# Gate and value products of three hidden blocks moved between the attention stages of the first half chunk, with fewer identity products

## The chip, the cores and the metric

The kernel runs on one core of one Trainium2 chip. The metric is the device time of one execution in microseconds (us); the median of three runs of the kernel before is 1180.62. The engines are named PE (TensorE, the matrix products), DVE (VectorE), ACT (ScalarE), POOL (GpSimd) and SP (SyncE, which issues the DMAs here). Each works through its own queue in order.

## What is computed

Eight sequences of 512 local and 32 global tokens, eight heads of 64. A local token attends to the local tokens within 32 places and to the global tokens; a global token attends to all. The output of attention, 4608 tokens of 512 numbers, goes through a gated feed-forward layer with 1536 hidden numbers:

```python
s_ll = np.where(mask, s_ll, -1000000000.0)
s_l = np.concatenate([s_lg, s_ll], axis=-1)
out_l = np.matmul(sm(s_l), np.concatenate([v_g, v_l], axis=2))
out_g = np.matmul(sm(s_g), v_all)
...
gate = 1.0 / (1.0 + np.exp(-(x @ w_gate)))
val = x @ w_val
return (gate * val @ w_out).astype(np.float32)
```

The three weights are given as 64-bit floats.

## The kernel before

The tokens are worked in chunks: the first sequence in two half chunks of 256 tokens (chunk 0 and chunk 1), the other sequences as chunks of 512, the global tokens as a last one. For each chunk attention makes x, and `ffn_stream` then runs over items (chunk, f), where f is one of 12 blocks of 128 hidden numbers. An item takes 12 gate products and 12 value products (hi times hi, lo times hi, hi times lo, each over four tiles kt of the 512 inputs, since numbers are split in a high and a low part), then tanh, minimum, exponential and merging on ACT and DVE, which give hh; then the output products with wo into the PSUM banks bank_o. The order of items begins with blocks 0 to 7 of chunk 0, then blocks 0 to 7 of chunk 1, then both by turns.

The order of everything is written by hand as a table of events with due times. `ffn_stream` yields after each step with the step's length in units of four products of 512 columns, and the events whose time has come are written out between. Events with times far below zero come before the first item: the attention of chunk 0 runs from -1000 on, four units for each head. A scheduler then moves instructions a little by its own estimate, within the dependences.

Attention of one head in chunk 0 (`local_unit`) has four stages: the scores on PE (L234) with the mask and minimum on DVE (L248) and the exponential on ACT (L251); the normalization on DVE (L218); the transposes on PE (L270), with a copy on ACT (L278); the products with v on PE (L293, L294), with a copy to x on ACT (L297). After every second head `x_split` (L372, L373) makes the high and low part of one kt tile of x. In chunk 0 `fill` adds products of the identity matrix with itself (L110) after the scores, after the transposes and after the products with v; nobody reads them.

The weights are converted on the chip. `stage` loads 512 KB of 64-bit words into one of three buffers; `convert` makes 32-bit floats of them (ACT L137, DVE L139 and L140), casts them to the high part (ACT L141) and subtracts for the low part (POOL L142), then stages the third load after it. Gate and value weights stay in SBUF; those for the output go to DRAM (L153, L154) and come back as wo for each item (L428). Their high and low parts share two buffers (tag kl). `CONVERT_EARLY` sets the times of block 0's three conversions, `CONVERT` the first time and the step of the others.

## Time and profile before

| | us |
|---|---|
| median of 3 runs | 1180.62 |
| lowest and highest | 1178.43, 1186.85 |
| the profiled execution | 1179.81 |
| its span, from the first to the last instruction | 1177.9 |

The profile is of one execution. A row of its timeline has the start and the length in us, engine, line, operation, what is written from what, the shapes and the count, and in brackets the idle time of the engine before it with what ended that. A product of 32-bit floats that are not split stands as two records. A row on DMAs has the count, the size of each and the median time from issue to landing. PE counts as busy while a product is on its way, so a busy PE isn't PE at its peak. The granted clock of PE is 1.00 throughout.

### The profile page before, as it was taken

The numbers are of one execution on the slowest core, as the hardware profiler recorded it, in microseconds if no ns is written. First come the engines' busy times: TensorE is split into PE (matmuls) and PEld (weight loads), VectorE is DVE, ScalarE is ACT, GpSimd is POOL, SyncE is SP. The second block draws the span as 40 slices with busy tenths as digits, with TensorE's granted clock in tenths as the row PEclk, the third lists the DMA queues.
The fourth block names the chain that finished last, engine by engine and source line by source line (L and its number), as shares of the span: only waits on it lengthen the run. The fifth ranks groups of instructions, "written<-read, shape, count | busy, mean of one in ns | idle before, by whom it ended". The sixth has DMA issues, their size and how long they took to land.

```text
span 1177.9 us, 19115 instructions
## 1 busy us (share of the span) xinstructions
PE 1146.4 (97%) x6596; PEld 962.3 (82%) x6596; DVE 773.7 (66%) x2132; ACT 753.2 (64%) x1737; POOL 413.3 (35%) x408
## 2 busy tenths in 40 slices
PE   8999999999999999999999999999999999999998
PEld 7777788888888888888888888888888888888897
DVE  5677657577676677667676677667676677533343
ACT  5898877566675676666675676666675675532343
POOL 2444435334353444334352444334452443100000
PEclk9999999999999999999999999999999999999999
DMA  8888844333443343343343343343344342122143
GB/s 295 283 288 279 259 134 128 95 116 94 115 116 113 106 115 98 106 140 90 113 115 114 105 116 98 107 149 91 103 116 122 99 118 81 44 100 72 54 151 118
DMA packets 59489, 151.81 MB, mean 129 GB/s; under 512 B 6144, under 2 KB 19456, under 8 KB 59392
## 3 DMA queue, kind: packets, MB, share of 16 engines
q1 hardware_dynamic: 59392, 150.59, 42.2%
q8 instruction: 52, 0.85, 0.3%
q14 instruction: 45, 0.37, 0.1%
HBM read 135.36 MB, written 15.20 MB: 128 GB/s over the span
## 4 chain that ended last, share of the span: by engine, by line
PE 75%; DVE 11%; ACT 8%; issue 3%; DMA 2%; POOL 1%; SPq 0%; ACTq 0%; DVEq 0%; POOLq 0%
PE bank_v L400 20%; PE bank_g L400 19%; PE bank_o L437 19%; PE bank_x L234 4%; DVE p_buf L218 4%; PE bank_y L270 4%; ACT s_sb L251 3%; PE bank_x L301 2%; PE bank_x L302 2%; PE bank_x L318 2%; PE bank_x L361 1%; DVE bank_v L420 1%; DVE bank_v L421 1%; PE bank_o L110 1%; ACT hh L423 1%
## 5 line engine op out<-in xcount | busy, mean ns | idle before, releaser
L400 PE MATMUL bank_v<-xt,wv 128*128 128x512 f32 (+1 forms) x1440 | 328.3, 364 | 14.1 <-DVE pt L282 14.1
L400 PE MATMUL bank_g<-xt,wg 128*128 128x512 f32 (+1 forms) x1440 | 330.4, 364 | 0.1
L437 PE MATMUL bank_o<-wo,hh 128*128 128x512 f32 x1224 | 329.2, 400 | 1.2 <-ACT hh L423 1.2
L400 PEld LDWEIGHTS bank_v<-xt,wv 128*128 128x128 f32 x1440 | 237.1, 189 | 51.0 <-issue 16.0
L400 PEld LDWEIGHTS bank_g<-xt,wg 128*128 128x128 f32 x1440 | 236.8, 189 | 37.4 <-issue 2.5
L437 PEld LDWEIGHTS bank_o<-wo,hh 128*128 128x128 f32 x1224 | 217.2, 189 | 41.8 <-ACT hh L423 3.0
L251 ACT ACTIVATE s_sb<-s_sb,nm 128x192 f32<-128x192 f32 (+1 forms) x240 | 110.4, 462 | 98.2 <-DVE nm L248 97.3
L218 DVE TENSOR_SCALAR p_buf<-s_sb,r 128x128 f32<-128x128 f32 (+2 forms) x443 | 153.5, 383 | 6.6 <-PE bank_y L270 1.7
L306 POOL TENSOR_TENSOR x<-t 64x256 f32<-64x256 f32 x104 | 76.4, 735 | 172.1 <-DVE t L305 146.1
L211 POOL TENSOR_TENSOR vhl<-v_raw,vhl 128x512 fp32r<-128x512 f32 x52 | 67.2, 1293 | 187.4 <-ACT vhl L210 104.1
L198 POOL TENSOR_TENSOR kl<-qk_raw,qk_hi 128x704 fp32r<-128x704 f32 x52 | 88.6, 1703 | 108.3 <-ACT qk_hi L197 107.8
L423 ACT CAST hh<-bank_v 128x512 fp32r<-128x512 f32 (+1 forms) x120 | 62.7, 522 | 96.1 <-DVE bank_v L421 95.2
L408 ACT ACTIVATE th<-bank_g 128x512 f32<-128x512 f32 (+1 forms) x120 | 63.7, 531 | 87.0 <-PE bank_g L400 86.6
L413 DVE TENSOR_SCALAR mn<-bank_g 128x512 f32<-128x512 f32 (+1 forms) x108 | 67.4, 624 | 71.8 <-ACT th L408 71.8
L305 DVE TENSOR_TENSOR t<-bank_x,t 64x512 f32<-64x512 f32 x104 | 70.7, 680 | 62.0 <-ACT t L304 61.1
L420 DVE TENSOR_TENSOR bank_v<-bank_v,mn 128x512 f32<-128x512 f32 (+1 forms) x120 | 73.6, 614 | 53.5 <-PE bank_v L400 48.4
L248 DVE CUSTOM_DVE_ANT_0 s_sb<-bank_x,masks 128x192 f32<-128x192 f32 (+1 forms) x240 | 79.9, 370 | 38.5 <-PE bank_x L234 35.6
L424 DVE TENSOR_TENSOR hh<-bank_v,hh 128x512 fp32r<-128x512 f32 (+1 forms) x120 | 73.0, 608 | 35.1 <-ACT hh L423 33.2
L200 POOL TENSOR_TENSOR qk_hi<-qk_raw,qk_hi 64x256 fp32r<-64x256 f32 x104 | 80.3, 792 | 4.1
L421 DVE SCALAR_TENSOR_TENSOR bank_v<-th,bank_v 128x512 f32<-128x512 f32 (+1 forms) x120 | 73.2, 610 | 1.8
L414 ACT ACTIVATE mn<-mn 128x512 f32<-128x512 f32 (+1 forms) x108 | 62.9, 583 | 12.9 <-DVE mn L413 8.2
L270 PE MATMUL bank_y<-ident,p_buf 128*128 128x128 f32 x440 | 69.7, 274 | 1.3 <-ACT mn L410 0.5
(108 smaller groups left out, 1648.7 us busy)
## 6 DMA issues: line engine op xcount, KB each, us to landing
wo<-wo_dram SPq DMA_DIRECT2D x116, 512.0 KB, 3.4
qk_raw<-in_qk_dram SPq DMA_DIRECT2D x104, 312.0 KB, 4.4
v_raw<-in_v_dram SPq DMA_DIRECT2D x52, 256.0 KB, 2.6
out_dram<-ob SPq DMA_DIRECT2D x34, 256.0 KB, 2.9
xt<-in_w_gate_dram SPq DMA_DIRECT2D x12, 512.0 KB, 5.4
xt<-in_w_val_dram SPq DMA_DIRECT2D x12, 512.0 KB, 5.0
xt<-in_w_out_dram SPq DMA_DIRECT2D x12, 512.0 KB, 5.3
v_nat<-in_v_dram SPq DMA_DIRECT2D x8, 512.0 KB, 7.6
```

What stands on the lines that cost most here:

```text
L198: nc.gpsimd.tensor_tensor(kl, t[:, K0:Q1], hi[:, K0:Q1].bitcast(F32), op=ALU.subtract)
L200: nc.gpsimd.tensor_tensor(hi[64:128, r], t[64:128, r], hi[64:128, r].bitcast(F32), op=ALU.subtract)
L218: nc.vector.tensor_scalar(out, in_, by, None, op0=ALU.mult)
L248: anchor[0] = nc.vector.tensor_tensor_reduce(out=s_sb[:, i, w], in0=s_ps[:, i, w], in1=mid[:, w], scale=-0.125, scalar=3.0e38, op0=ALU.add ...
L251: exp_at[0] = nc.scalar.activation(s_sb[:, i, w], s_sb[:, i, w], AF.Exp, bias=nm[:, i:i + 1], scale=-1.0, accum_out=sm[:, i:i + 1])
L270: nc.tensor.transpose(pt_ps[:, t], flat[:, t * P:(t + 1) * P], ident)
L306: nc.gpsimd.tensor_tensor(dst, t0[:, :, 0], t0[:, :, 1], op=ALU.add)
L400: nc.tensor.matmul(acc, w[a][:, t, fs], xt[:, c, t, x0:x0 + ntok], start=n == 0, stop=n == 11)
L420: nc.vector.tensor_tensor(acc, acc, mn, op=ALU.mult)
L421: nc.vector.scalar_tensor_tensor(acc, th, 1.0, acc, op0=ALU.add, op1=ALU.mult)
L423: nc.scalar.copy(hh[:, 0, 0:ntok], acc)
L437: nc.tensor.matmul(o_ps[t], ph[:, a, t * P:(t + 1) * P], pwo[:, c], start=f2 == 0 and i == 0, stop=f2 == NF - 1 and i == 2)
```

## The change

Line numbers move: L110 becomes L112, L137 L156, L139 and L140 L158 and L159, L141 L160, L142 L161, L153 and L154 L172 and L173, L218 L237, L234 L254, L248 L269, L251 L272, L270 L291, L278 L297, L293 and L294 L312 and L313, L372 L389, L400 L478, L428 L430, L437 L447. The new line L409 is a product of a portion.

- `fill` is called twice only: two products at the start and seven after the scores of head 1, tied behind given instructions. Before, it was eight at the start and one after each of three stages of each head.
- For blocks 0, 1 and 2 of chunk 0 gate and value products are taken out of `ffn_stream`. `pre_products` writes them in portions of six (one kt tile: three gate products, three value products), each tied behind the last attention product written before it. A portion goes into one bank, gate in one half and value in the other: block 0 in bank_o2, block 1 in bank_o3, block 2 in bank_o1. At the start a product with a tile of zeros clears each of them.
- `ffn_stream` begins with the gating of these three blocks (`gate_parts`, `merge`), then item 3; the output products of blocks 0 and 1 come after item 3's gate products, those of block 2 after its value products. Each item from 3 to 20 yields 0.5 more.
- The conversions stand in a new order: gate and value of blocks 0, 1, 2 first (`PRE_AT`), their output weights later (`PRE_OUT`), and from block 3 on by `CONVERT`, which begins one unit earlier at block 3 where it began with block 0. The loads follow that order.

```diff
-FILL = (8, 1)
+FILL = (2, 7)
-CONVERT = (-2, 4, 1, 3)
-CONVERT_EARLY = (-985, -980, -977)
+CONVERT = (-3, 4, 1, 3)
+PRE = 3
+PRE_AT = (-992.9, -991.5, -987.5, -985, -983.2, -979.2)
+PRE_OUT = (-971.5, -967.5, -2)
...
+    zero = spl.tile([P, 512], F32R, name="zero", tag="kl")
+    nc.vector.memset(zero.bitcast(F32), 0.0)
+    pre_banks = []
+    for i in (2, 3, 1)[:PRE]:
+        bank = ps.tile([P, 2, 256], F32, name=f"bank_o{i}")
+        nc.tensor.matmul(bank.rearrange("p a c -> p (a c)"), zero[:, 0:P], zero, start=True, stop=False)
+        pre_banks.append(bank)
+    last_fill = fill(FILL[0])
...
-        if T["first"]:
-            fill(FILL[1])
+        if T["first"] and h == 1:
+            with tc.issue_after(m.ins):
+                fill(FILL[1])
...
+    def pre_products(f, kt):
+        C = chs[0]
+        ntok, x0, xt = C["ntok"], C["x0"], C["xt"]()
+        fs = slice(f * P, (f + 1) * P)
+        bank = pre_banks[f]
+        for i, w in enumerate((wg, wv)):
+            for n, (a, c) in enumerate(((0, 0), (1, 0), (0, 1))):
+                with tc.issue_after(pe_at[0].ins):
+                    nc.tensor.matmul(bank[:, i], w[a][:, kt, fs], xt[:, c, kt, x0:x0 + ntok],
+                                     start=False, stop=kt == KT - 1 and i == 1 and n == 2)
...
+    def load_wo(f):
+        t = ffn.tile([P, 2, DM], F32R, name="wo", bufs=2)
+        nc.sync.dma_start(t.bitcast(F32), wo_dram[f])
+        return t
...
+        wos = {f: load_wo(f) for f in range(2)}
+        for f in range(PRE):
+            half = slice(256 * (f % 2), 256 * (f % 2) + 256)
+            bank = pre_banks[f]
+            hh = hhs[f // 2][:, :, half]
+            gate_parts(bank[:, 0], th[:, half], mn[:, half], f % 2)
+            merge(bank[:, 1], th[:, half], mn[:, half], hh)
+            pend.append((chs[0], f, hh, lambda f=f: wos[f]))
+        for n_it in range(PRE, len(items) + 1):
...
+                        if n_it == PRE:
+                            yield from out(False)
+                            wos[2] = load_wo(2)
+                            yield from out(False)
...
+            if n_it < 7 * PRE:
+                yield 0.5
...
+    for t_, f, kind in order:
+        queue.append((t_, 4, (lambda f=f, k=kind: convert_w(f, k)) if kind < 2 else (lambda f=f: convert_wo(f))))
+    for f in range(PRE):
+        for kt in range(KT):
+            at = (-982.95, -981.95, -978.9)[f] + 8 * kt if kt < KT - 1 else -962.4
+            queue.append((at, 5, lambda f=f, kt=kt: pre_products(f, kt)))
```

PE, the middle of chunk 0's attention, from the transposes of head 2 to the scores of head 5, before (bank_x holds scores and products with v, bank_y transposes, p_buf and p_first the weights of attention):

```order
L270 MATMUL bank_y<-ident,p_buf 128x128 x4
L234 MATMUL bank_x<-qk_nat 128x192
L234 MATMUL bank_x<-qk_nat 128x224
L110 MATMUL bank_o_124<-ident 128x128
L293 MATMUL bank_x<-pt_nat,v_nat 64x128
L294 MATMUL bank_x<-pt_nat,v_nat 64x128
L293 MATMUL bank_x<-pt_nat,v_nat 64x128
L294 MATMUL bank_x<-pt_nat,v_nat 64x128
L270 MATMUL bank_y<-ident,p_first 128x128 x4
L234 MATMUL bank_x<-qk_nat 128x192
L234 MATMUL bank_x<-qk_nat 128x224
L110 MATMUL bank_o_124<-ident 128x128 x4
```

The same engine now, from within the first portion of block 0, which follows head 2's products with v, to the product with the low value weights in block 1's first portion (wg_108 and wv_110 are high parts, wg_109 and wv_111 low ones; bank_o_127 is block 0's bank, bank_o_129 block 1's):

```order
L409 MATMUL bank_o_127<-xt,wg_108 128x256
L409 MATMUL bank_o_127<-xt,wv_110 128x256
L409 MATMUL bank_o_127<-xt,wv_111 128x256
L409 MATMUL bank_o_127<-xt,wv_110 128x256
L291 MATMUL bank_y<-ident,p_first 128x128 x4
L409 MATMUL bank_o_129<-xt,wg_108 128x256
L409 MATMUL bank_o_129<-xt,wg_109 128x256
L409 MATMUL bank_o_129<-xt,wg_108 128x256
L254 MATMUL bank_x<-qk_nat 128x192
L409 MATMUL bank_o_129<-xt,wv_110 128x256
L254 MATMUL bank_x<-qk_nat 128x224
L409 MATMUL bank_o_129<-xt,wv_111 128x256
```

In the place of fillers stand portions, and both halves of head 5's scores stand between products that read weights of block 1.

ACT, the stretch around head 4's exponentials, before (L137 and L141 are steps of a conversion):

```order
L278 COPY pt_nat<-bank_y 128x512
L372 CAST xt<-x_204 128x256
L137 ACTIVATE xt<-xt 128x512
L251 ACTIVATE s_first,sm<-s_first,nm 128x192
L251 ACTIVATE s_first,sm<-s_first,nm 128x224
L297 COPY x_281<-bank_x 64x256
L141 CAST wg_108<-xt 128x4x128
L278 COPY pt_first<-bank_y 128x512
```

And now:

```order
L160 CAST wg_108<-xt 128x4x128
L156 ACTIVATE xt<-xt 128x512
L272 ACTIVATE s_first,sm<-s_first,nm 128x192
L272 ACTIVATE s_first,sm<-s_first,nm 128x224
L160 CAST wv_110<-xt 128x4x128
L156 ACTIVATE xt<-xt 128x512
L314 COPY x_304<-bank_x 64x256
L297 COPY pt_first<-bank_y 128x512
L156 ACTIVATE xt<-xt 128x512
```

The conversion that began ahead of head 4's exponentials was the first of all; now it is the fourth, and the fifth and sixth begin right behind it.

SP, from the stores of block 0's output weights to those of block 1, before (wo_dram_112 to 115 are blocks 0 to 3):

```order
L153 DMA wo_dram_112<-wo_hi 128x512
L154 DMA wo_dram_112<-wo_lo 128x512
L126 DMA xt<-in_w_gate_dram 128x4x256
L126 DMA xt<-in_w_val_dram 128x4x256
L428 DMA wo<-wo_dram_112 128x1024
L126 DMA xt<-in_w_out_dram 128x1024
L153 DMA wo_dram_113<-wo_hi 128x512
```

And now, from the stores of block 2 on, with those of blocks 0 and 1 ahead of these rows:

```order
L172 DMA wo_dram_114<-wo_hi 128x512
L173 DMA wo_dram_114<-wo_lo 128x512
L145 DMA xt<-in_w_out_dram 128x1024
L430 DMA wo<-wo_dram_112 128x1024
L172 DMA wo_dram_115<-wo_hi 128x512
L173 DMA wo_dram_115<-wo_lo 128x512
L430 DMA wo<-wo_dram_113 128x1024
```

The loads of wo for blocks 0 and 1 stand behind the stores of blocks 2 and 3.

More of the change, by code (lines that the diff above doesn't have):

```diff
@@ L233, in local_unit @@
                 js = slice(k0 + j * BLK + w0, k0 + j * BLK + w1)
-                nc.tensor.matmul(s_ps[:, i, w0:w1], qj, kt[:, js], start=t == 0, stop=t == last)
-        if T["first"]:
-            fill(FILL[1])
+                with tc.issue_after(last_fill.ins) if T["first"] and h == 0 else nullcontext():
+                    m = pe_at[0] = nc.tensor.matmul(s_ps[:, i, w0:w1], qj, kt[:, js], start=t == 0, stop=t == last)
+        if T["first"] and h == 1:
+            with tc.issue_after(m.ins):
+                fill(FILL[1])
         if T["first"]:
@@ L446, in ffn_stream @@
-            prev = (C, f, hh, wo) if n_it < len(items) else None
+                    wo = load_wo(f)
+            if pend:
+                yield from out(n_it >= len(items))
+            if n_it < len(items):
+                pend.append((C, f, hh, wo))
+            if n_it < 7 * PRE:
+                yield 0.5
     def att_events(ci, start, per, tail=0):
@@ L531 @@
         queue.append((9 * NF * (ci - 2) + (START["x2"] if ci == 2 else 0), -1, new_x))
[L532 to L538 removed]
+    for t_, f, kind in order:
+        queue.append((t_, 4, (lambda f=f, k=kind: convert_w(f, k)) if kind < 2 else (lambda f=f: convert_wo(f))))
[3 more added lines that the diff above has]
+            queue.append((at, 5, lambda f=f, kt=kt: pre_products(f, kt)))
     queue.append((-1002, 2, lambda: [stage(i) for i in range(3)]))
```

116 lines of the change are left out of this document (58 added, 58 removed).

## The prediction

> **What bounds the kernel now.** I read the page first, then the busy time by stretches, then the order of time on PE, ACT and SP in the first 60 us, since the change touches nothing later than that. The page says that PE is hardly ever free:
>
> ```profile
> span 1177.9 us, 19115 instructions
> PE 1146.4 (97%) x6596; PEld 962.3 (82%) x6596; DVE 773.7 (66%) x2132; ACT 753.2 (64%) x1737; POOL 413.3 (35%) x408
> PE 75%; DVE 11%; ACT 8%; issue 3%; DMA 2%; POOL 1%; SPq 0%; ACTq 0%; DVEq 0%; POOLq 0%
> ```
>
> Three quarters of the chain that ends last is PE, so the end moves by what PE's in-order queue loses or gains, and little else. The start differs. By stretches (PE, PEld, DVE, ACT, POOL busy, clock, DMA share, GB/s):
>
> ```profile
> 10.00:20.00 10.00, 10.00 (x67) 7.69 (x67) 4.88 (x26) 5.63 (x16) 0.73 (x1) 1.00 1.00 364
> 30.00:40.00 10.00, 8.30 (x59) 6.71 (x59) 7.83 (x21) 8.31 (x21) 6.01 (x6) 1.00 0.82 264
> 60.00:100.00 40.00, 38.33 (x283) 29.08 (x282) 29.25 (x74) 36.09 (x98) 18.39 (x16) 1.00 0.87 281
> ```
>
> From 10 to 20 us the DMA engines are full (1.00) while ACT is half idle. From 60 to 100 us ACT is busy 36.09 of 40 us and PE 38.33 of 40: both are near their limit. Part of PE's work before 36 us is filler:
>
> ```profile
> 3.75 1.76 PE L234 MATMUL bank_x<-qk_nat 64*128 64x192 f32 x8 [3.75 <-DMA qk_nat<-in_qk_dram]
> 5.44 6.11 PE L110 MATMUL bank_o<-ident 128*128 128x128 f32 x34
> 11.39 0.38 PE L270 MATMUL bank_y<-ident,p_buf 128*128 128x128 f32 x2
> 28.46 1.60 PE L110 MATMUL bank_o<-ident 128*128 128x128 f32 x12
> 30.00 0.43 PE L293 MATMUL bank_x<-pt_first,v_nat 128*64 128x128 f32 x2
> 32.69 0.43 PE L293 MATMUL bank_x<-pt_nat,v_nat 128*64 128x128 f32 x2 [1.03 <-ACT pt_nat L278]
> 35.04 0.43 PE L293 MATMUL bank_x<-pt_first,v_nat 128*64 128x128 f32 x2 [0.68 <-ACT pt_first L278]
> 36.06 0.61 PE L400 MATMUL bank_g<-xt,wg 128*128 128x256 f32 x3
> 36.61 0.97 PE L234 MATMUL bank_x<-qk_nat 64*128 64x224 f32 x4
> 37.50 1.34 PE L400 MATMUL bank_g<-xt,wg 128*128 128x256 f32 x9
> 38.68 1.12 PE L400 MATMUL bank_v<-xt,wv 128*128 128x256 f32 x8
> 39.73 1.05 PE L318 MATMUL bank_x<-qk_nat 64*32 64x256 f32 x4
> 53.38 1.20 PE L437 MATMUL bank_o<-wo,hh 128*128 128x512 f32 x4
> 7.51 0.87 DVE L218 TENSOR_SCALAR p_buf<-s_first,r 128x128 f32<-128x128 f32 x4
> ```
>
> Head 0's weights are ready at 7.51 + 0.87 = 8.38, but its transposes start at 11.39, behind 17 fillers (34 records). Attention of the first half chunk ends where the first gate product starts, at 36.06.
>
> **The change part by part.** The span is 1177.9, the profiled execution 1179.81, 0.8 under the median of 1180.62; the sum is made against 1179.81.
>
> *Fillers.* At the start seven instead of 17 stand between head 0/1's scores and the first transposes: 14 records at 34 in 6.11, 0.18 each, end at about 8.1, so the transposes can start when their input is ready: 11.39 - 8.4 = 3.0 less; I take 2.8, since three zero products and two fillers now stand ahead of the first scores. Those are hidden by the wait for qk (3.75 in the first row); without that cover they cost their length, five products of at most 0.4, some 2 us. The 15 later fillers (30 records) go: 12 records hold PE from 28.46 to 30.00, 0.128 each, so 3.8.
>
> *Waits for ACT at the end of attention.* The 1.03 and 0.68 after the copies at L278 go, 1.7, since other work stands there now.
>
> *Portions.* 72 products of 256 columns move from behind 36.06 to between the heads; no product is saved. One costs (38.68 - 37.50)/9 = 0.131, a portion of six 0.8. What must be early for them is the weights: six conversions instead of three stand inside attention, and each first instruction of a conversion (Prelu, L137) waits in ACT's in-order queue for a load, with the exponentials and copies of the heads behind it. Loads and the ACT steps (issue, landing after so many us, then ACT in order of time):
>
> ```profile
> 9.91 0.38 SPq L183 DMA_DIRECT2D v_nat<-in_v_dram  x1
> v_nat<-in_v_dram SPq DMA_DIRECT2D x1, 512.0 KB, 9.5
> 2.12 0.51 SPq L126 DMA_DIRECT2D xt<-in_w_gate_dram  x1
> xt<-in_w_gate_dram SPq DMA_DIRECT2D x1, 512.0 KB, 7.8
> 19.66 0.44 ACT L251 ACTIVATE s_first<-s_first,nm 128x192 f32<-128x192 f32 x1
> 21.34 0.57 ACT L278 COPY pt_first<-bank_y 128x512 f32<-128x512 f32 x1
> 29.36 0.46 ACT L251 ACTIVATE s_first<-s_first,nm 128x192 f32<-128x192 f32 x1
> 30.27 0.66 ACT L137 ACTIVATE xt<-xt 128x512 f32<-128x512 f32 x1
> 33.41 0.61 ACT L141 CAST wg<-xt 128x512 fp32r<-128x512 f32 x1
> 33.92 0.37 ACT L297 COPY x<-bank_x 64x256 f32<-64x256 f32 x1
> 34.41 0.58 ACT L278 COPY pt_first<-bank_y 128x512 f32<-128x512 f32 x1
> 21.51 1.37 POOL L142 TENSOR_TENSOR wg<-xt,wg 128x512 fp32r<-128x512 f32 x1 [1.50 <-ACT wg L141]
> ```
>
> The first weight lands at 2.12 + 7.8 = 9.9; in the new order head 0's copy stands behind its Prelu, so that copy is at about 10.5. The fourth weight (value, block 1) is issued behind the v_nat load that lands at 9.91 + 9.5 = 19.4; with its own 512 KB at 364 GB/s (1.4) it lands at 20.8. Its Prelu (0.66) stands ahead of head 4's exponentials: 21.4, against 19.66 before. The two weights of block 2 follow behind one more load of qk, near 23.5 and 25. From there I go down the new ACT order with these spacings: two exponentials 0.91 (29.36 to 30.27), a cast 0.5 (33.41 to 33.92), a copy of x 0.5, Prelu 0.6; and POOL's 1.37 after each cast, for which PE waits at the low half of the weight. Head 3's copy comes to some 24.5 (21.34 before), head 7's to 38 (34.41), and the last portion ends at about 43.7. Before, the same products would have been done at 36.06 + 75 x 0.131 = 45.9. So PE is 2.2 ahead there. In terms: -2.8 - 3.8 - 1.7 and new waits of +6.1. Bounds of the new waits: 2, if the fourth weight lands early and only POOL's 1.37 shows, and 10, if all three late weights cost their lateness one after the other.
>
> *First output products.* In the new PE order the output products of block 0 follow gate products of block 3 and two score groups, about 4.7 after block 0's last portion (12 and 9 products at 0.131, scores 0.89 from 36.61 to 37.50, global scores 1.05). What they need is late. The load of wo (L428, now in load_wo) stands in SP's queue behind the stores of wo block 2, whose cast stands in ACT's queue behind block 0's tanh; block 1's load stands behind the stores of block 3. hi and lo of wo have two buffers, so each cast and each POOL subtraction waits until the store before it has landed:
>
> ```profile
> wo_dram<-wo_hi SPq DMA_DIRECT2D x1, 256.0 KB, 4.6
> wo_dram<-wo_lo SPq DMA_DIRECT2D x1, 256.0 KB, 2.4
> wo<-wo_dram SPq DMA_DIRECT2D x1, 512.0 KB, 5.7
> xt<-in_w_gate_dram SPq DMA_DIRECT2D x1, 512.0 KB, 3.4
> ```
>
> (These are the stores issued at 28.74 and 52.11, the load at 43.52, and a free-queue load at 20.58.) From block 0's last portion: tanh and cast 0.8, POOL 1.37, store and a stage load 0.7, and the load 4 gives 6.9 for block 0; for block 1 one more store (3.5, between 2.4 and 4.6), POOL 1.37, and a load gives about 12. PE would be there at 4.7 + six output products at 0.25 (the row at 53.38 has four, with 1.03 to the next), 6.2. So PE waits about 6. Bank o1, which block 0's second output tile needs, also holds block 2's sums until block 2 is merged, and that is about as late. Behind PE's wait stand the transposes and scores of the second half chunk, and ACT's copies for them. Bounds: 0, if stores and loads land so soon that both are there (the wait is between ends far apart; I take 6 because ACT has some twenty steps at about 0.4 between block 0's tanh and block 2's merge, which gives nearly as much without any DMA), and 9 with the landings of 4.6 and 5.7 throughout.
>
> [...]
>
> *Relief.* By the new order 26 conversions instead of 20 stand ahead of the end of the second half chunk's attention, so ACT has less to do after that, and DMA too. PE's waits from 45 to 140 us, in total, times, longest:
>
> ```profile
> PE bank_o L437 <- ACT hh L423: 1.2, 3, 0.6
> PE bank_y L320 <- DVE mn L413: 0.6, 1, 0.6
> PE bank_y L270 <- ACT mn L410: 0.5, 1, 0.5
> PE bank_y L270 <- DVE p_buf L218: 0.4, 1, 0.4
> ```
>
> They come to 2.7; I let them go, and the bounds are 0 and 2.7. The added half steps of the stream move attention against products, and no work. Sum: 1179.8 - 2.8 - 3.8 - 1.7 + 6.1 + 6.0 - 2.7 = 1180.9, and I say 1180.5, as the second wait is the one likelier too long than too short.
>
> **The rivals.**
> Output weights in time: the stores land in 2.4 and less, or ACT gets to wo sooner; then 6 of the sum goes: 1174.5. For it: the 2.4 above. Against: ACT's queue, as above. Chance 0.25.
> ACT bounds the start up to 140 us rather than PE: ACT has 36.09 of 40 busy. Then only the idle ACT time that the change fills counts, about 3 us of the half-idle 10 to 20 us: 1177. Against: PE is 38.33 of 40. Chance 0.12.
> The clock falls: 24 fillers go and PE now waits 2 to 4 us at a time. The first row of fillers runs at 0.18 a record, the later at 0.128: PE starts slower than it goes later. If two waits each bring the slow pace back for some 4 us of work, at a third to a half of it lost, that is about 4: 1184.5. For it: the waits at the fourth weight and at the output products are the longest since 3.75. Against: fillers or products end 2 to 3 us before. [...] Chance 0.10.
> Slower: loads queue. If the three late weights keep the 7.8 to 9.5 us of the first 10 us rather than 3.4, each Prelu holds ACT, and the heads behind it, some 4 to 5 longer, 12 together: 1192.5. It decides from a landing of about 7 on, for loads issued after 11. Against: 3.4 for the load at 20.58. Chance 0.06.
>
> **How the numbers follow.** The forecast has 0.47, the rivals 0.25, 0.12, 0.10 and 0.06. A measurement of this kernel can tell about 1% from no change, 11.8 us. Faster by that would need every gain (11.0) and no new wait, and more: 0.04. Slower: nearly the last rival, 0.05. Within: 0.91. The range takes in the first three rivals with the small bounds of the portions (1172) and the clock with the large ones (1188); the likeliest case alone has 1176 to 1187.
>
> **What would show it.** Right: transposes of head 0 at about 8.5 to 9; ACT waiting for a load in front of head 4's exponentials, until about 21; last portion near 44; PE waiting some 6 us for wo or bank o1 near 46 to 55; the waits from 60 to 140 smaller. Wrong: no wait at the output products (then 1174), a doubled duration of products after a wait (the clock), or the last portion after 48.

## The result, and the profile after

The changed kernel took 1196.97 us in the median of four runs (1194.12 to 1199.3) against 1180.86 (1178.43 to 1186.85): a ratio of 1.0125 between the runs, with a 95% interval of 1.0099 to 1.015. I had said 1180.5, no change, and 1172 to 1188; the medians are 16 us apart, and the time is outside the range. The profiled execution is the one of 1194.12. The page:

```profile
span 1192.1 us, 19011 instructions
PE 1150.7 (97%) x6553; PEld 963.4 (81%) x6553; DVE 772.9 (65%) x2133; ACT 756.4 (63%) x1737; POOL 414.3 (35%) x408
PE 78%; DVE 11%; ACT 7%; issue 2%; DMA 2%; POOL 1%; SPq 0%; ACTq 0%; DVEq 0%
```

PE is busy 4.3 us longer than before (1150.7 against 1146.4) with fewer instructions: part of its work goes at a slower pace. The busy time by stretches (PE, PEld, DVE, ACT, POOL, clock, DMA share, GB/s) shows where:

```profile
10.00:20.00 10.00, 8.38 (x52) 6.17 (x52) 7.86 (x30) 7.83 (x20) 4.33 (x4) 1.00 1.06 398
20.00:30.00 10.00, 8.06 (x34) 5.29 (x31) 9.16 (x29) 7.35 (x20) 4.53 (x5) 0.83 0.81 271
30.00:40.00 10.00, 8.38 (x60) 7.08 (x61) 8.10 (x24) 7.74 (x21) 4.21 (x4) 1.00 0.87 289
50.00:60.00 10.00, 4.42 (x13) 2.96 (x11) 7.50 (x21) 8.15 (x25) 5.04 (x4) 0.58 0.90 301
60.00:100.00 40.00, 39.01 (x260) 29.20 (x259) 23.32 (x76) 35.41 (x99) 13.59 (x13) 0.98 0.82 272
220.00:230.00 10.00, 7.86 (x46) 6.74 (x45) 7.92 (x23) 7.59 (x19) 5.38 (x5) 0.83 0.23 81
```

The clock, 1.00 throughout before (mean 1.000), is 0.83, 0.58 and again 0.83 in three of these rows. Inside a row it is either whole or half: the trace's clock records have half speed from 24.25 us for 3.41 us, from 51.55 for 10.24, from 198.33 and 225.63 for 3.41 each. Such a drop to half speed is called a fall below.

PE's order of time in the first phase and at the first output products:

```profile
2.24 1.65 PE L120 MATMUL bank_o<-zero 128*128 128x512 f32 x3 [2.24 <-DVE zero L116]
4.67 1.77 PE L254 MATMUL bank_x<-qk_nat 64*128 64x192 f32 x8
6.37 2.20 PE L112 MATMUL bank_o<-ident 128*128 128x128 f32 x14
8.78 0.33 PE L291 MATMUL bank_y<-ident,p_buf 128*128 128x128 f32 x1 [0.21 <-DVE p_buf L237]
14.35 0.43 PE L312 MATMUL bank_x<-pt_first,v_nat 128*64 128x128 f32 x2 [1.00 <-ACT pt_first L297]
22.73 0.39 PE L409 MATMUL bank_o<-xt,wv 128*128 128x256 f32 x1 [1.10 <-ACT wv L160]
46.38 0.52 PE L409 MATMUL bank_o<-xt,wv 128*128 128x256 f32 x3
49.88 0.22 PE L337 MATMUL bank_y<-qk_nat 64*32 64x32 f32 x2
54.41 0.77 PE L447 MATMUL bank_o<-wo,hh 128*128 128x512 f32 x1 [4.30 <-ACT pg_buf L340]
56.45 2.50 PE L447 MATMUL bank_o<-wo,hh 128*128 128x512 f32 x5 [1.28 <-DVE hh L426]
```

Head 0's transposes start at 8.78 instead of 11.39. The view puts the 4.30 us at 54.41 down to an ACT copy (L340, from 54.20 to 54.37) that these products don't read. What they need is block 0's wo, and its load, issued at 49.69, lands at 54.27:

```profile
49.69 0.45 SPq L430 DMA_DIRECT2D wo<-wo_dram  x1
wo<-wo_dram SPq DMA_DIRECT2D x1, 512.0 KB, 4.6
```

The experiment e2 below moves this load, and the wait goes. Five output products then take 2.50 us, 0.50 each, where four took 1.20 before: half speed. ACT's order of time at the late weight, head 4's exponentials and head 3's copy:

```profile
19.69 0.69 ACT L156 ACTIVATE xt<-xt 128x512 f32<-128x512 f32 x1 [0.52 <-DMA xt<-in_w_val_dram]
21.13 0.46 ACT L272 ACTIVATE s_first<-s_first,nm 128x192 f32<-128x192 f32 x1 [0.75 <-DVE nm L269]
23.40 0.58 ACT L297 COPY pt_first<-bank_y 128x512 f32<-128x512 f32 x1
```

The loads of the three late weights, issued at 11.72, 15.50 and 18.54 us, have these sizes and times to landing:

```profile
xt<-in_w_val_dram SPq DMA_DIRECT2D x1, 512.0 KB, 8.0
xt<-in_w_gate_dram SPq DMA_DIRECT2D x1, 512.0 KB, 6.7
xt<-in_w_val_dram SPq DMA_DIRECT2D x1, 512.0 KB, 5.0
```

PE's waits from 60 to 140 us (total, times, longest), and three rows of its order of time in the attention of chunk 2:

```profile
PE bank_x L312 <- ACT pg_buf L339: 1.2, 1, 1.2
PE bank_y L291 <- DVE p_buf L237: 0.9, 1, 0.9
PE bank_o L447 <- DMA wo<-wo_dram: 0.6, 1, 0.6
PE bank_y L357 <- DVE pg_buf L237: 0.4, 1, 0.4
...
197.80 0.75 PE L478 MATMUL bank_v<-xt,wv 128*128 128x256 f32 x4 [2.41 <-DVE pt L301]
225.40 0.35 PE L318 MATMUL bank_x<-pt,vhl 128*128 128x256 f32 x1 [1.85 <-DVE pt L301]
227.75 1.78 PE L478 MATMUL bank_g<-xt,wg 128*128 128x256 f32 x8
```

The waits from 60 to 140 us come to 3.1 us, not less than the 2.7 before (from 45 to 140), and near 200 and 225 us new ones stand, with half speed behind them: the eight products at 227.75 take 1.78 us; eight took 1.12 before.

To see where the time goes I give each PE instruction its usual time in the trace of before (start to next start) and add that up as work; products that nobody reads (identity products, products of zeros) are no work. The lag is then how much later than the kernel before the same amount of work is done, by the one traced execution of each kernel. For all work behind 221 us it stays the same within about 1 us. In us, at six places, for the kernels spoken of below:

```
time in the kernel before   46.4   53.4   90.9  141.0  180.2  220.9
the changed kernel          -0.9    6.9    6.9    7.8    8.1   14.0
e2                           1.9    3.2   12.6   14.6   15.0   19.2
e3                          -3.3   -3.3   -3.3   -3.9   -2.3   -2.3
e13                         -1.6    5.9    5.9    7.8    8.2   13.0
e14                         -1.6   -0.9    6.9   10.8   11.1   16.0
e15                         -1.6   -0.9    5.3    8.2    8.6   14.0
e16                         -1.3    0.1    2.8    9.3    9.7   14.7
e18                          4.2    4.2    4.5    3.8    4.9    4.9
```

The last column can be read off rows, within 0.3 us. The same 20 products start at 220.82 before, at 235.12 in the changed kernel and at 234.81 in e15:

```profile
220.82 1.36 PE L361 MATMUL bank_x<-vhl,ptg 128*64 128x128 f32 x20
235.12 1.36 PE L378 MATMUL bank_x<-vhl,ptg 128*64 128x128 f32 x20
234.81 1.36 PE L386 MATMUL bank_x<-vhl,ptg 128*64 128x128 f32 x20
```

And by kind, PE's time from its first instruction up to the last of these places (identity: with the three products of zeros at the start; half clock: what the work done at half speed took more; rest: what is left of the time, with the products of zeros at the waits of chunk 2 in it):

```
                     work  identity  idle  half clock  rest    sum
the kernel before   174.0    10.3     8.8     0.0      24.1   217.2
the changed kernel  174.0     4.6    20.3     8.3      25.5   232.8
e3                  174.0     3.0    12.0     1.7      24.1   214.8
e11                 174.1     9.4    15.8     1.7      30.8   231.8
e15                 174.1    13.5    14.5     0.0      30.6   232.7
e18                 174.0     4.4    15.4     6.3      24.3   224.3
```

So in this execution the change saves 5.7 us of dummy products at the start, adds 11.5 of idle time, and loses 8.3 to half clock. (PE's first instruction comes 1.5 us earlier than before, so the lag is that much less than the difference of the sums.)

Four theories stood against each other. A: the clock follows PE's work, so a wait costs twice. B: the waits alone cost the time, and the clock falls whatever PE does. C: the attention of chunks 1 and 2 comes late. D: the chain of attention on ScalarE and VectorE bounds this phase, so that a faster PE only waits longer.

### The profile page after: what moved, and what is told of

It reads as the page before. It is cut to its first block, busy times and chain, and to the rows that moved or that the text cites. A ratio compares the mean times of both kernels' runs of the same rounds, so it can differ in the third digit from the quotient of the medians.

```text
span 1192.1 us, 19011 instructions
## 1 busy us (share of the span) xinstructions
PE 1150.7 (97%) x6553; PEld 963.4 (81%) x6553; DVE 772.9 (65%) x2133; ACT 756.4 (63%) x1737; POOL 414.3 (35%) x408
## 4 chain that ended last, share of the span: by engine, by line
PE 78%; DVE 11%; ACT 7%; issue 2%; DMA 2%; POOL 1%; SPq 0%; ACTq 0%; DVEq 0%
PE bank_o L447 20%; PE bank_v L478 20%; PE bank_g L478 20%; PE bank_x L254 4%; PE bank_y L291 4%; DVE p_buf L237 4%; ACT s_sb L272 2%; PE bank_x L335 2%; PE bank_x L318 2%; PE bank_x L319 2%; PE bank_x L378 1%; DVE bank_v L424 1%; DVE bank_v L423 1%; PE bank_x L312 1%; ACT hh L425 1%
## 5 line engine op out<-in xcount | busy, mean ns | idle before, releaser
L478 PE MATMUL bank_v<-xt,wv 128*128 128x512 f32 (+1 forms) x1404 | 323.1, 367 | 16.6 <-DVE pt L301 16.6
L447 PE MATMUL bank_o<-wo,hh 128*128 128x512 f32 x1224 | 332.5, 402 | 6.3 <-ACT pg_buf L340 4.3
L478 PE MATMUL bank_g<-xt,wg 128*128 128x512 f32 (+1 forms) x1404 | 326.1, 367 | 0.9 <-DVE pt L301 0.9
L478 PEld LDWEIGHTS bank_v<-xt,wv 128*128 128x128 f32 x1404 | 233.0, 190 | 54.2 <-issue 19.0
L478 PEld LDWEIGHTS bank_g<-xt,wg 128*128 128x128 f32 x1404 | 232.9, 190 | 36.3 <-issue 1.9
L447 PEld LDWEIGHTS bank_o<-wo,hh 128*128 128x128 f32 x1224 | 218.2, 190 | 47.3 <-ACT pg_buf L340 4.4
L272 ACT ACTIVATE s_sb<-s_sb,nm 128x192 f32<-128x192 f32 (+1 forms) x240 | 110.6, 463 | 97.2 <-DVE nm L269 96.4
L237 DVE TENSOR_SCALAR p_buf<-s_sb,r 128x128 f32<-128x128 f32 (+2 forms) x443 | 151.0, 377 | 6.3 <-PE bank_y L291 1.0
L269 DVE CUSTOM_DVE_ANT_0 s_sb<-bank_x,masks 128x192 f32<-128x192 f32 (+1 forms) x240 | 80.2, 370 | 32.9 <-PE bank_x L254 30.4
L291 PE MATMUL bank_y<-ident,p_buf 128*128 128x128 f32 x440 | 72.0, 279 | 1.4 <-DVE p_buf L237 1.4
```

Source lines behind the costliest of these rows:

```text
L237: anchor[0] = nc.vector.tensor_scalar(out, in_, by, None, op0=ALU.mult)
L269: anchor[0] = nc.vector.tensor_tensor_reduce(out=s_sb[:, i, w], in0=s_ps[:, i, w], in1=mid[:, w], scale=-0.125, scalar=3.0e38, op0=ALU.add ...
L272: exp_at[0] = nc.scalar.activation(s_sb[:, i, w], s_sb[:, i, w], AF.Exp, bias=nm[:, i:i + 1], scale=-1.0, accum_out=sm[:, i:i + 1])
L291: pe_at[0] = nc.tensor.transpose(pt_ps[:, t], flat[:, t * P:(t + 1) * P], ident)
L447: nc.tensor.matmul(C["o"][t], hh[:, a, t * P:(t + 1) * P], (wo() if callable(wo) else wo)[:, c], start=f == 0 and i == 0, stop=f == NF - 1 ...
L478: nc.tensor.matmul(acc, w[a][:, t, fs], xt[:, c, t, x0:x0 + ntok], start=n == 0, stop=n == 11)
```

## The experiments

e3, e8 and e12 are edits of the kernel before, all others of the changed kernel. Each ratio is against runs of the kernel before that were made along with it.

### Does the clock follow PE's idle time? (e8)

```diff
+STALLS = {n: (n // 3 + n // 12) % 4 for n in range(27, 99, 3) if n % 12}
...
+                        if n_it in STALLS:
+                            for k in range(STALLS[n_it]):
+                                a = th[:, 0:384] if k == 0 else st.bitcast(F32)
+                                nc.gpsimd.tensor_tensor(st, a, a, op=ALU.subtract)
+                            zl, zr = (st[:, 0:P], st) if STALLS[n_it] else (th[:, 0:P], pg[:, KALL:])
+                            with tc.issue_after(m.ins):
+                                hold = nc.tensor.matmul(C["o"][0][:, 0:zr.shape[1]], zl, zr, start=False, stop=False)
```

> The kernel before, with 18 waits put into its long steady part, where the clock is 1.00 throughout: behind the gate products of 18 blocks TensorE waits for the block's tanh (5 of them) or for 1, 2 or 3 subtractions of 384 columns on GpSimd behind it (about 1 us each), and adds a product of zeros. Theory A: waits that leave a 3.41 us stretch with less than about 0.45 of full work (over 1.9 us of one stretch idle) are followed by a stretch at half clock, which costs about 1.7 us beside the wait; the shortest (under 1.9 us) never, those over 3.8 us always, those between by where the grid falls. Theory B: the clock does not follow these waits; the time grows by the waits alone.

1241.61 us in one execution. Two waits of the same length, as PE's order of time has them, and the stretches around them by the windows of e8 (columns as above):

```profile
346.42 0.53 PE L426 MATMUL bank_o<-st 128*128 128x384 f32 x1 [1.92 <-POOL st L423]
914.78 0.44 PE L426 MATMUL bank_o<-st 128*128 128x384 f32 x1 [1.92 <-POOL st L423]
...
343.20:346.60 3.40, 1.48 (x7) 0.93 (x6) 1.23 (x4) 2.08 (x4) 2.18 (x3) 1.00 0.35 133
346.60:350.00 3.40, 3.40 (x11) 2.71 (x12) 0.88 (x4) 0.48 (x1) 0.00 (x0) 0.51 0.28 76
...
913.20:916.60 3.40, 1.82 (x10) 1.55 (x11) 0.30 (x2) 0.54 (x2) 1.53 (x2) 1.00 0.29 77
916.60:920.00 3.40, 3.40 (x23) 2.84 (x22) 2.36 (x5) 1.51 (x4) 0.00 (x0) 1.00 0.00 0
```

The first wait lies in one stretch of the 3.41 us grid, which is left with 1.48 us of busy PE; the next stretch goes at half speed (0.51). The second is cut by the grid; 1.82 us stay, and nothing falls. The lag grew by 3.8 us at the first, by 2.4 at the second. (The share of full work is the time that a stretch's products take at whole clock, over its 3.41 us; it is less than the busy share, since a product on its own counts for more: by the rows above one product of a portion is busy for 0.39 us at 22.73, three in a row for 0.52 at 46.38.) Of the 13 waits for GpSimd, the seven whose stretch held 0.08 to 0.39 of full work were followed by half speed, the six with 0.47 or more (one of 2.99 us, halved by the grid) were not. Beyond its wait a place cost about 0.5 us without a fall and about 2 with one, so a fall costs 1.4 to 1.5, near the 1.7 expected. The rest of the 61.7 us that this run took longer is neither (the 13 waits are 26.6 us in all); it stays unexplained. Theory A's rule holds in this execution, and B is out, since the clock followed planted waits.

The executions agree: those of the changed kernel have 1194.12 us at a mean clock of 0.991, 1196.25 at 0.989, 1197.69 at 0.988, 1199.3 at 0.987. A thousandth of clock is 1.2 us of span, and the times follow it nearly one for one (5.2 us over four thousandths). Each kernel has one trace, so where the slower executions fell isn't shown. The grid stands at another offset in each trace (a fall's start, less whole stretches of 3.413 us, leaves 0.4 us in the changed kernel, 0.8 in e5, 0.7 in e6), so it is likely that the same kernel falls at other places from one execution to the next.

### Holding the clock (e1, e5, e6, e7, e11)

e1 puts products that do nothing into the wait at the first output products; e11 does so at all four places where the clock fell. e5 to e7 put the identity products back behind every stage of the first phase; e5 adds e1's, e6 the early loads of e2 (below) in their place, and e7 is e5 with products of zeros at the two waits of chunk 2:

```diff
+                            with tc.issue_after(last_g.ins):
+                                last_f = fill(WARM)
                             yield from out(False)
...
+            if (f, kt, i) == (1, 0, 0):
+                with tc.issue_after(last_p.ins):
+                    fill(4)
...
+                    if (n_it, nm) in ((17, "bank_g"), (20, "bank_v")):
+                        for k in range(8):
+                            with tc.issue_after(last_g.ins):
+                                last_z = nc.tensor.matmul(C["o"][k % 2], zc, wo[:, 0], start=False, stop=False)
```

(The first piece is e1's with WARM = 24, and e11's with 18; the others are e11's.)

> Theory A (half clock): the 3.4 us and more of half clock after the first output products come because TensorE stands idle before them. 24 identity products (about 0.18 us each, 4.3 us together) fill that idle time, so nothing waits longer, but the granted clock stays 1.00 from 50 to 70 us, and the time falls by 3 to 4 us against the changed kernel, to about 1193. Theory B (waits alone, the clock falls at those places whatever TensorE does): clock again near 0.6 between 50 and 60, time 1196 to 1198. Theory C (late attention) expects no change of its own between 188 and 228 us.

1195.78 us, 1.0123 [1.0103, 1.0143]. PE's order of time and the windows of e1:

```profile
51.54 5.52 PE L112 MATMUL bank_o<-ident 128*128 128x128 f32 x48
...
50.00:60.00 10.00, 9.40 (x67) 7.69 (x65) 9.38 (x25) 9.06 (x27) 3.28 (x3) 1.00 0.82 280
60.00:70.00 10.00, 10.00 (x61) 7.31 (x60) 4.25 (x18) 7.80 (x22) 4.07 (x4) 1.00 0.90 319
```

From 50 to 70 us the clock stays up as A says, but the median is 1.2 us under the changed kernel's, not the 3 to 4 expected, and lies just under B's range. The 24 products take 5.52 us, not 4.3, and the output products follow at 57.54 instead of 54.41; in the profiled execution there is a second fall at 31.94 us as well.

> The changed kernel with identity products back behind every attention stage of the first phase (8 at the start, 2 behind each set of scores, transposes and value products) and 24 ahead of the first output products. Theory A (the clock is granted by how much TensorE did in the 3.41 us stretch before; in the records so far a stretch with less than about 0.45 of full work is followed by one at half speed): granted clock 1.00 up to 190 us; the four half-speed stretches of the changed kernel before 62 us held 4.4 us worth of full-speed work, so 1190 to 1194 against 1197, with the two drops of chunk 2 (198 and 225 us) still there. Theory D (attention's chain on ScalarE and VectorE bounds the first 230 us, so a faster TensorE only waits longer): 1195 to 1199 although the clock is 1.00 up to 190 us.

1200.36 us, 1.0169 [1.0152, 1.0186]. This is slower than either theory had it. The fillers take 17.6 us up to the place where the kernel before is at 46.4 (10.3 there), and the lag there is already 11 us. The clock still fell at 28.13, 52.02 and 232.93 us, so A's condition, a whole clock up to 190 us, was not reached.

> The same fillers of the first phase, without those ahead of the output products, and the early loads and other banks of e2. Theory A: e2 lost its gain to half clock from 22 to 36 and from 60 to 74 us (nine half-speed stretches, some 13 us of full-speed work in 31 us); with the first of them gone and the output wait gone, 1186 to 1191; the granted clock from 20 to 40 us is 1.00. Whether the low stretch at 56 to 60 us comes again hangs on where the grid of stretches falls. Theory D: 1195 to 1199.

1199.41 us, 1.0167 [1.0152, 1.0182], again above both ranges, with falls at 27.96 (6.8 us), 62.10, 82.58 and 232.76 us.

> e5 with 12 more products of zeros (512 columns, about 0.23 us each) into the open sums at each of the two waits of chunk 2 (after item 17's gate products and after item 20's value products). Theory A: clock 1.00 in all windows up to 260 us; 2 to 4 us less than e5. If the drops at 198 and 225 us aren't made by the waits ahead of them: the clock falls there all the same and the time is 0 to 2 us above e5. Theory D: no gain, 0 to 3 us above e5.

1200.09 us, 1.0173 [1.0158, 1.0188]. In the profiled execution (0.999) no fall is left behind 34 us, so chunk 2's falls do come from its waits. But nothing is won by it: between the work of 180 and 221 us it loses 4.9 us, e5 4.2, the changed kernel 5.9. The products of zeros stand there in the place of half clock, and the median is e5's.

> The changed kernel with products that do nothing, no more of them than the waits hold, at the four places where the clock fell: 4 identity products ahead of block 1's first value portion, 18 ahead of the first output products, 8 products of zeros at each of the two waits of chunk 2. Theory A: mean clock 0.997 or more; by the ledger of the two traces 8.3 us of the loss is half clock, and the added products take some 2 us more than the idle time that they fill: 1189 to 1192. Theory D (no gain from the clock): 1196 to 1200 although the clock is up.

1193.51 us, 1.0115 [1.0094, 1.0135]; the two executions at 0.999 have 1191.22 and 1192.25. D's 1196 to 1200 is out, and the median lies 1.5 us above A's range. The median is 3.5 us under the changed kernel's, but as ratios to the kernel before 1.0115 and 1.0125 are 1 us apart, and their intervals overlap. So of the 8.3 us of half clock little came back: in the ledger they became dummy products and other idle time.

### The wait at the first output products (e2, e13, e14, e15)

```diff
-        wos = {f: load_wo(f) for f in range(2)}
+    wos = {}
+    queue.append((-3.5, 9, lambda: wos.update({f: load_wo(f) for f in range(2)})))
...
-        chs.append(dict(ntok=len(blocks) * P, x0=blocks[0] * P, o0=blocks[0], first=ci == 0,
+        chs.append(dict(ntok=len(blocks) * P, x0=blocks[0] * P, o0=(2, 0, 0)[min(ci, 2)], first=ci == 0,
```

> The loads of the first two output weights move ahead of the stores of the third and fourth, and chunk 0's sums take the banks of blocks 0 and 1. Theory A: the wait of 6.2 us at the first output products goes down to 1 us or less, and with it the half clock of 54 to 62 us (3.5 us): 8 to 9 us less at equal work by 62 us, 1188 to 1189 at the end. Theory B: only the wait goes, 1190.5 to 1191.5. Theory C: the attention of chunk 1, which stands behind these products, comes about 8 us earlier and the loss of 6 us between 188 and 228 us shrinks as well: 1183 to 1186.

1198.97 us, 1.0147 [1.0115, 1.0179]: nothing is won, and all three theories had it lower. The lag grows by 1.3 us over the output products instead of 7.8, so the wait is gone, and then by 9.4 up to 91 us. The windows of e2:

```profile
50.00:60.00 10.00, 7.52 (x34) 4.64 (x33) 8.80 (x24) 8.62 (x28) 3.19 (x3) 1.00 0.79 266
60.00:70.00 10.00, 10.00 (x38) 7.46 (x36) 4.04 (x11) 6.69 (x17) 2.56 (x2) 0.50 0.77 257
70.00:80.00 10.00, 8.50 (x39) 5.53 (x37) 6.81 (x19) 6.17 (x17) 3.36 (x3) 0.82 0.52 159
```

The clock now falls behind the mended place, for 13.65 us. To take that away, e13 joins e11 and e10 (below); e14 differs from e13 in e2's edit (and nine identity products behind the output products instead of 18 ahead of them); e15 adds six identity products behind the global scores of four heads.

> e11 with the loads of e10 (attention loads of chunk 1 behind the six early weights). The two gained about 3.5 and 2 us; theory A: together 1188 to 1192, mean clock 0.997 or more. It is the partner of the next run, which differs only in the output weights.

1190.59 us, 1.009 [1.0073, 1.0107], as A said: about 4 us less than the changed kernel by the ratios. Three of its executions have a clock of 1.000 and took 1189.27 to 1190.70 us. The executions of the kernel before at 1.000 in the same round took 1178.35 to 1179.83. So with a whole clock on both sides some 11 us of the loss remain.

> The run before with the early loads of the output weights and the other banks of e2, so that the wait of 6.2 us at the first output products goes, and with 9 identity products behind these products instead of 18 ahead of them. If e2 gave nothing only because the clock fell behind the place mended (theory A), the clock is now held from 55 to 75 us and the time is 4 to 6 us under its partner: 1183 to 1187. If the wait was one for attention's chain, which comes to light at the next place (theory D): within 2 us of its partner, with TensorE's waits for exponentials and copies of chunk 1 between 58 and 100 us grown by 4 us or more.

1194.93 us, 1.013 [1.0115, 1.0145]: above its partner. The lag is -0.9 us behind the output products (e13: 5.9) and 6.9 at 91 us (e13: 5.9). The clock fell from 69.3 for 10.2 us, so this alone decides nothing.

> e14 with 6 identity products (about 0.12 us each) behind the global scores of heads 1 to 4 of chunk 1, 2.9 us in all, ahead of the waits of 1.4 and 0.7 us at 66.6 and 70.4 us after which e14's clock fell for 10.2 us. Theory A: clock 1.00 from 50 to 105 us; at 98 us the kernel is 3 to 5 us behind the kernel before instead of 6.9, and the end comes at 1187 to 1191 against 1190.6 for e13 and 1194.9 for e14. Theory D: the clock is up, but the waits for exponentials and copies of chunk 1 grow by as much, and the end is at 1191 to 1195.

1193.21 us, 1.0105 [1.007, 1.014]. There is no half clock in the profiled execution before its last 2 us and no wait at the output products, and the lag still goes from -0.9 to 5.3 at 91 us and 14.0 at 221. Of A's numbers the clock came; the end is D's. But PE's waits did not grow as D has it: idle time from 52 to 189 us is 4.5 us (e13: 4.7), beside 7.8 of dummy products.

### The place of attention and the loads (e4, e10, e16, e17)

```diff
-START = dict(per0=4, base1=1, per1=1.1, base2=23, per2=3, x2=28, lead=8, native_heads=4)
+START = dict(per0=4, base1=-5, per1=1.1, base2=23, per2=3, x2=28, lead=8, native_heads=4)
```

(e16 and e17; e4 has base2=17 instead. e10 ties the loads of chunk 1 behind the sixth weight's: `with tc.issue_after(stage_ins[5].ins) if T["native"] == 2`.)

> The changed kernel with chunk 2's attention due 6 units of FFN work (about 6 us) earlier. Theory C: the loss between 188 and 228 us shrinks from 6 to 0 to 3 us, and the granted clock in 190 to 230 us rises over 0.95: 1191 to 1194. Theories A and B as far as the start goes: nothing changes before 60 us (lag about 7 us there), and if the loss of 188 to 228 us isn't from the attention's place: 1195 to 1199.

1200.64 us, 1.0169 [1.0148, 1.0189]. The falls at 198 and 225 us go, as C says, but come back at 121.8 and 142.3 us, where this attention meets that of chunk 1 and the conversions; the lag is 18 us at 141.

> The changed kernel with the attention loads of chunk 1 put behind the loads of the six early weights. Theory A: the second value weights land about 4 us earlier than 19.67 us, TensorE's wait of 1.1 us at 22.7 us goes and the stretch before 24 us, which held 0.30 of full work, rises above 0.45: no half clock before 45 us, 1193 to 1196. Rival: chunk 1's first scores then wait for their loads, 1197 to 1201.

1194.81 us, 1.0118 [1.0096, 1.0139]. The end lies in A's range, with the lag at 46.4 us at -1.9, but it is not clear of the changed kernel's 1.0125, and the fall that A wanted gone, at 23.8 us, stayed.

> e13 without the 18 identity products ahead of the output products, and with chunk 1's attention due 6 units of FFN work earlier (base1 -5 instead of 1), so that its first two heads stand ahead of item 3's gate products and of the output products, and fill TensorE's wait for the output weights. If the loss comes from chunk 1's attention standing behind these products (theory D: it starts 17 us later than in the kernel before and ScalarE's and VectorE's work comes late with it): first transposes of chunk 1 near 48 us instead of 59, and 1184 to 1188. If attention without FFN work beside it leaves TensorE empty (theory A: the clock falls there): 1190 to 1196, clock under 0.8 between 45 and 60 us.

1192.58 us, 1.0097 [1.008, 1.0114]. Chunk 1's first transposes stand at 47.8 us, the wait at the output products is filled with attention, and the lag at 91 us is only 2.8. It is 9.3 at 141: the idle time comes later, with falls at 111 and 138 us. The end lies in A's range, though the clock did not fall where A had it.

> e15 (early output weights, identity products that hold the clock) with the same earlier attention of chunk 1. Theory D: 4 to 7 us under e15, 1186 to 1189, clock 0.998 or more. Otherwise 1191 to 1195.

1192.68 us, 1.0104 [1.0076, 1.0131]: what was expected if D does not hold, 0.5 us under e15.

### One part of the change alone (e3, e9, e18, e12)

e3 is the kernel before with `FILL = (2, 7)` and the diff's ties on `fill`. e9 is the changed kernel with `PRE = 2`. e18 has the change's conversions and identity products without portions:

```diff
-PRE = 3
+PRE, PREW = 0, 3
-CONVERT = (-3, 4, 1, 3)
+CONVERT = (10, 4, 1, 3)
...
-    order = [(PRE_AT[k], k // 2, k % 2) for k in range(2 * PRE)] + [(PRE_OUT[f], f, 2) for f in range(PRE)]
+    order = [(PRE_AT[k], k // 2, k % 2) for k in range(2 * PREW)] + [(PRE_OUT[f], f, 2) for f in range(PREW)]
```

> The kernel before with nothing but its identity products thinned: 2 at the start, 7 behind head 1's scores. As the prediction had it, 6.6 us of TensorE work go and nothing takes their place: 1173 to 1176. Theory A: with so little work TensorE's clock falls below 0.9 in at least one of the 10 us windows before 45 us and half or more of that is lost: 1177 to 1183. Theory B: clock 1.00, 1173 to 1176.

1179.13 us, 0.9987 [0.9974, 1.0001]. At full clock it has 1175.33 and 1177.23, about 3 us less than the kernel before at full clock and under half of the prediction's 8.3. In seven of ten executions the clock is 0.998 or less. The end is A's, but not its place: in the profiled execution the clock is whole up to 137 us. So the thinning is worth about 3 us where the clock holds, and little in the median.

> The changed kernel with two blocks in portions instead of three (PRE = 2; the third comes in the stream as before). Only one set of output products then stands ahead of the attention of chunk 1, and no sums of a third block lie in the bank that they want. If waits and the falls of the clock that they bring carry the loss (theory A), both shrink: 1184 to 1192, mean clock 0.993 or more. If the loss comes from having taken FFN work out of the cover of chunk 1's and chunk 2's attention (theory C), it is about two thirds of that of three blocks: 1190 to 1193 whatever the clock does.

1192.6 us, 1.0106 [1.0085, 1.0127]: in C's range and just above A's, with falls at five places before the end; it does not tell the two apart.

> The changed kernel with its thinned identity products and its early conversion of the first three blocks' weights (same places in the first phase), but without portions: all gate, value and output products run in the stream, in the order of the kernel before, and the later blocks' conversions keep the pace of the kernel before. If the six early conversions on ScalarE, VectorE and GpSimd hold up attention and carry the loss (theory D): chunk 0's last transposes at 38 to 40 us as in the changed kernel (33.7 before), and 1186 to 1194. If the loss comes from the portions and what follows from taking them out of the stream: within 4 us of e3, 1177 to 1183.

1183.98 us, 1.0023 [1.0012, 1.0035]. PE's order of time in e18, then in e3, at head 3's value products:

```profile
24.23 0.69 PE L312 MATMUL bank_x<-pt_first,v_nat 128*64 128x128 f32 x2 [3.67 <-ACT pt_first L297]
38.25 0.66 PE L291 MATMUL bank_y<-ident,p_first 128*128 128x128 f32 x4
...
29.66 0.66 PE L271 MATMUL bank_y<-ident,p_first 128*128 128x128 f32 x4
```

ACT's copy comes late, as in the changed kernel, and head 7's transposes stand at 38.25 instead of 29.66: in the first phase D's sign came. In this execution half the clock was granted from 23.20 for 13.65 us, but one execution at 0.999 took 1183.07, so the end isn't the clock's. Behind the first phase the lag stays at 4 to 5 us: the early conversions alone cost 4.2 us (1.0023 against 0.9987 of 1180 us) and nothing later. The end lies between the two expectations; most of the change's loss is not theirs.

e18 leaves out more than the portions. It has no half steps of the stream, the gate, value and output products in the old order, and, by its `CONVERT`, the later blocks' conversions at the old pace. ACT's first steps of conversions, counted up to the end of chunk 1's attention (its last x_split, at 93.99 us before, at 110.12 in the changed kernel, at 98.54 in e18, in this order):

```profile
L137 ACT ACTIVATE xt<-xt 128x512 f32<-128x512 f32 x21 | 13.7, 670 | 0.0
L156 ACT ACTIVATE xt<-xt 128x512 f32<-128x512 f32 x27 | 17.8, 670 | 0.6 <-DMA xt<-in_w_val_dram 0.5
L156 ACT ACTIVATE xt<-xt 128x512 f32<-128x512 f32 x22 | 14.5, 673 | 2.0 <-DMA xt<-in_w_gate_dram 1.2 <-DMA xt<-in_w_val_dram 0.8
```

So what separates e18 from the changed kernel is the portions together with six, and not one, further conversions ahead of that attention's end. No run takes these apart.

> e3 (the kernel before with thinned identity products) with 8 products of zeros (256 columns, about 0.12 us each) between the gate and value products of item 10, just ahead of the waits of 1.2 us that left the stretch from 133.8 us at 0.46 of full work. Theory A: the fall at 137 us goes in most executions, so the median comes to what e3 shows at full clock: 1176 to 1178, against about 1179.1 for e3 and 1180 for the kernel before. Otherwise 1179 to 1181.

1186.02 us, 1.0053 [1.004, 1.0066]. This is above both expectations. Behind the 1.12 us of added products a wait of 2.74 us for VectorE's part of the gate ends at 143.65, and the clock fell at 143.1 us. No version faster than both kernels was found but e3, whose 0.13% its interval does not tell from none.

## Why the prediction was wrong, step by step

- **Fillers and the first transposes (-2.8, -3.8, -1.7).** Right in kind, and too large: the ledger has 5.7 us less, the products of zeros counted in, but the first scores start at 4.67 instead of 3.75 us, since the three zero products wait for their memset until 2.24. I had held them to be hidden. All three terms were 8.3 together; e3, which has the thinning alone, shows 3.3 in one execution.
- **Portions (+6.1).** The chain was right: the fourth weight's Prelu at 19.69 (forecast landing 20.8), head 4's exponentials at 21.13 (21.4), head 3's copy at 23.40 (24.5). The last portion ended about 3 us late, at 46.9 (43.7), behind waits like that of 1.10 and a stretch of half clock; the lag there is -0.9 instead of -2.2. e18 and e3 show what is inside, in one execution each: the conversions cost about 7.5 us of lag by then (4.2 against -3.3; e18's long stretch of half clock lies within them), and the portions win 5 of them back.
- **First output products (+6.0).** PE waits 4.30 and 1.28, 5.6 in all, for the two causes given, the late wo and then bank o1, held until block 2 is merged (the hh at 56.45). The size is nearly right. But the lag grew by 7.8, as half clock came with the wait. And the step's premise, that this wait is the price, did not hold: taken away (e2, e14, e15) most of its time comes back within 40 us.
- **Relief (-2.7, and nothing at all behind 140 us).** This is the step that failed. The waits up to 140 us did not shrink (3.1 us against 2.7), and from 53 to 180 us the lag grows by 1.2. From 180 to 221 us, where I had put nothing since "the change touches nothing later", it grows by 5.9. Against the forecast these are 3.9 and 5.9 us of the 13 that this execution came out later; the portions are 1.3 and the output products 1.8. I let work that was done early count as won, and six conversions done early count as relief. The count was right (26 instead of 20; the traces have 27 instead of 21), but no relief came of it: chunk 1's attention begins 17 us later and takes hardly less time, 39.4 us from its first x_split to its last against 40.4, and ACT is as near its limit as before (from 60 to 100 us 35.41 of 40 us, against 36.09). The products of the portions, some 9 us, are those that stood beside the attention of chunks 1 and 2. e15, e16 and e17 are 7.6 to 9.3 us behind at 141 us, as are the changed kernel and e13 (7.8), whichever wait was mended, while e18, which has those products in the stream and the later conversions at the old pace, keeps its lag. That fits lost cover, and it fits the earlier conversions; which of the two it is, and which engine's steps set the pace, stays open.
- **The clock (rival, chance 0.10, 4 us).** The rival was named and its weight was wrong. I held falls unlikely since fillers or products end 2 to 3 us before the waits, though I expected a wait of 6 us at the output products myself. And the trace has a fall after a wait of 1.10 us: the stretch of the grid from 20.8 us held 0.30 of full work, and in e8 0.39 or less in a stretch was followed by half speed, 0.47 or more was not. The 4 us were my estimate; no run shows that a wait brings the slow pace back for some 4 us of work. The trace has half speed three times for 3.41 us and once for 10.24. The sign that I had named for it, a doubled duration of products after a wait, came, if not in full: from 56.45 us an output product takes 0.50 us, against 0.30 before. Six half-speed stretches cost 8.3 us in the profiled execution. But some 11 us of the loss remain where the clock is whole (e13), so the clock is the smaller part of it.
- **The other rivals.** Output weights in time was wrong: block 0's came at 54.27. Loads queueing had its condition in part: the three late loads took 8.0, 6.7 and 5.0 us rather than 3.4. But they landed at 19.7, 22.2 and 23.5 us, earlier than the forecast had them (20.8, 23.5 and 25), ACT waited only 0.52 us for the first (the row at 19.69), and the price of 12 us did not come. "ACT bounds the start" had the right thought, that PE's gain isn't the kernel's, and the wrong sign.

Put together from the ratios, as shares of 1180 us: thinner identity products -1.5 us (e3), early conversions of three blocks +4.2 (e18 less e3), and +12 (the changed kernel less e18) for the portions with their place in the stream and the earlier pace of the later conversions. Of these holding the clock gives back 1 us (e11), with the other order of loads 4 (e13).

## What to carry to other kernels

Work moved early out of a stream need not be won: ask which waits it stood beside, and what it covered there. Where the engine that bounds the kernel has spare time in the first phase, look at what the moved work needs from the others (here six conversions on ScalarE) before counting its own length. And look at what the clock does behind a new wait: of two waits of 1.92 us in e8 the one that half speed followed cost 3.8 us of lag, the other 2.4.

## What the runs showed of the hardware

The falls in the traces last 3.41 us or a whole multiple (6.8 in e6, 10.24 in the changed kernel, 13.65 in e2 and e18), and start whole multiples of 3.41 us apart within an execution (24.25, 51.55, 198.33 and 225.63 in the changed kernel), at another offset in each trace. In e8 up to 0.39 of full work in a stretch was followed by half speed, 0.47 and more was not. In e3 it was otherwise: half speed followed the stretch from 133.8 us, which held 0.46, and not the one from 24.6 us, which held 0.38. So my measure of work does not account for every fall. In e2 four half-speed stretches followed one another from 60 to 73.6 us; PE was busy in them all, with 0.41 to 0.48 of full work in each.
